# Splitting the first sums of a Strassen-Winograd token-pair product, and interleaving two accumulation chains

## The chip, the cores and the metric

The kernel runs on one core of one Trainium2 chip. The metric is the device time of one launch in microseconds (us), as the median of several runs of the same program. All traces are of single profiled executions of that program.

## The reference

Four batches, 8 heads of 40 features, 768 tokens. First an mLSTM cell over the tokens, then a block that mixes by a two-dimensional Fourier transform and ends in a small MLP. Only the MLP's second product is touched by the change:

```python
# x: (4, 768, 320), the mLSTM's output with the heads joined
X = np.fft.fft(np.fft.fft(x, axis=1), axis=2)
u = x + np.real(X)
un = (u - mean(u)) / np.sqrt(var(u) + 1e-06)          # over the 320 features
ch = np.maximum(un @ w_ch1, 0.0) @ w_ch2              # 320 -> 1280 -> 320
out = u + ch
```

## The kernel before

Everything is fp32. A token block is 128 tokens; a batch has six of them, in two groups (`gr` 0 and 1) of three. The whole program is one hand-written plan: `at(slot, phase, fn, args)` files a function under a slot and a phase, and `run()` calls them in sorted order, so the order on each engine is the order of these keys. Within a slot the phases are EVAC 0, FILL 1, MAIN 2, FILL_PE 3. The engines then run their own queues in order, and wait for each other on semaphores.

**First MLP product (the "sets").** For batches 1 to 3 `mlp_block` takes two of the ten hidden blocks of 128 features at a time, for both groups, as a 2x2 Strassen-Winograd scheme in four steps. There are five such sets, `i` = 0 to 4, so `mlp_block` fills four slots for each set and the last set ends at slot `s`. In a set TensorE fills four PSUM banks (line 897, the tails of the 320 features on line 902). ScalarE copies some of the results to the hidden tiles (lines 915, 919, 924), VectorE adds others onto them (`add`, line 906): one addition in step 1 and three at the end of step 3. The hidden tile of the fourth kind is written by ScalarE with its relu straight from PSUM (line 932). The other three kinds get their relu in place (`mlp_relu_in_place`, line 936), one after each of the next three slots, and after the last set all three in a row in slot `s`, phase EVAC.

The hidden tiles are `hid[gr, r]`, four of them, each holding five feature blocks (one for each set) by 384 tokens (three token blocks). `A11, A12, A21, A22` are the slices of `hid[1,1], hid[1,0], hid[0,1], hid[0,0]` for one pair of token blocks.

**Second MLP product (the "pairs").** `mlp_out_pair(b, n, step)` takes pair `n` of three: one token block of group 1 and one of group 0, again as a Strassen-Winograd scheme of seven products of five matmuls each (`product`, line 999, one matmul for each feature block, 128x160 out). They alternate between two PSUM banks: `x` is bank (n) % 2 and `y` is the other one. Step 0 makes two products straight from hidden tiles: A11 into `x` and A12 into `y`. Step 1 adds the product of the sum S2 onto `x`, and starts `y` anew with S1; step 2 adds S3 onto `x` and S4 onto `y`; step 3 adds A22 onto `x`. After each product VectorE takes the bank's contents onto the residual (`residual`, line 949), since every partial total is one that some output wants. So the next product on a bank waits for the residual before it, and VectorE's queue order decides when that is.

**The four sums.** `hidden_sums(n, which, f0, f1)` (line 985, VectorE) makes S1 = A21 + A22, S2 = S1 - A11, S3 = A11 - A21, S4 = A12 - S2 over the feature blocks `f0` to `f1`. For pairs 1 and 2 they are made whole (128x640), planned inside steps 2 and 3 of the pair before. For pair 0 they are made in two parts: blocks 0 to 3 (128x512) in the last set's steps, S1 and S2 ahead of the three additions of step 3 and S3 and S4 behind them; and block 4 (128x128) once the last relus are in.

Between the pairs' steps, batches 1 and 2 also run the next batch's work: Fourier products (`pz` line 686, `pu` line 729, `put` line 772) and the mLSTM (scores line 465, `mlstm_weigh` on VectorE line 471). After batch 3's sets there is nothing but pairs.

Of the kernel before, what the change touches and what calls it, by code (L numbers as in the profile page):

```python
# [26 lines left out]
NFF = DFF // L  # L27
# [23 lines left out]
def kernel(  # L51
# [33 lines left out]
    def bank(name, shape, n=None):  # L85

        return ps_m.tile(shape, FP, name=name, tag=f"pm{next(turn) if n is None else n}")
# [34 lines left out]
    def at(slot, phase, fn, *args):  # L122
        plan.setdefault((slot, phase), []).append((fn, args))
# [7 lines left out]
    EVAC, FILL, MAIN, FILL_PE = range(4)  # L131
# [813 lines left out]
    def residual(b, c, cols, po):  # L945

        k = mixes[b]
        u = k.u[:, c, cols]
        nc.vector.scalar_tensor_tensor(out=u, in0=po, scalar=k.rstd[:, c:c + 1], in1=u, op0=OP.mult, op1=OP.add)  # L949

    def store(b, c):
        nc.sync.dma_start(out=out[b, c * L:(c + 1) * L, :], in_=xs[b][:, c, 0:DM])
# [20 lines left out]
    def pair_block(n, gr, r):  # L973

        i = MLP_PAIRS[n][gr]
        return hid[gr, r].rearrange("p (f t) -> p f t", t=TG * L)[:, :, i * L:(i + 1) * L]
# [10 lines left out]
    def mlp_out_pair(b, n, step):  # L987

        k = mixes[b]
        half, first, last = NFF // 2, slice(0, HALF_D), slice(HALF_D, DM)  # L990
        c1, c2 = ORDER[TG + MLP_PAIRS[n][1]], ORDER[MLP_PAIRS[n][0]]
        if step == 0:
            k.po = [bank("po", [L, HALF_D], (n + j) % 2) for j in range(2)]
        x, y = k.po
        w = {(r, side): w2_sb[:, 1 - r:NFF:2, side * HALF_D:(side + 1) * HALF_D] for r in range(2) for side in range(2)}

        def product(po, a, w, start=False):
            for f in range(half):
                nc.tensor.matmul(po, a[:, f], w[:, f], start=start and f == 0, stop=f == half - 1, skip_group_check=True)  # L999

        def s(j):
            return hsum[f"S{j}"].rearrange("p (f t) -> p f t", t=L)

        if step == 0:
            product(x, pair_block(n, 1, 1), w[0, 0], True)
            residual(b, c1, first, x)
            product(y, pair_block(n, 1, 0), w[1, 0], True)
            residual(b, c1, first, y)
        elif step == 1:
            product(x, s(2), w2x["T2"])  # L1010
            residual(b, c1, last, x)
            product(y, s(1), w[0, 1], True)
            residual(b, c2, last, y)
        elif step == 2:
            product(x, s(3), w2x["T3"])
            residual(b, c2, last, x)
            product(y, s(4), w[1, 1])
            residual(b, c1, last, y)
            store(b, c1)
        else:  # L1020
            product(x, pair_block(n, 0, 0), w2x["T4"])
            residual(b, c2, first, x)
            store(b, c2)
# [3 lines left out]
    def plan_mlp(b, s):  # L1027
        groups = range(NT // TG)
        for i in range(NFF // 2) if b > 0 else ():
            for step in range(4):  # L1030
                at(s, MAIN, mlp_block, b, i, step)
                s += 1
            end = i == NFF // 2 - 1
            for n, (gr, f) in enumerate(((1, 2 * i + 1), (1, 2 * i), (0, 2 * i))):
                at(*((s, EVAC) if end else (s + n, MAIN + 0.5)), mlp_relu_in_place, gr, f)
        for gr in groups if b == 0 else ():
            for f in range(NFF):
                at(s, MAIN, mlp_in, b, gr, f)
                s += 1
                if f % 2:  # L1040
                    at(s, EVAC, mlp_relu, b, gr, f - 1)
                    at(s, EVAC, mlp_relu, b, gr, f)
        if b > 0:
            for j in range(1, 5):
                at(s - 1, FILL + 0.3 if j < 3 else FILL_PE + 0.3, hidden_sums, 0, (j,), 0, NFF // 2 - 1)
            at(s, EVAC, hidden_sums, 0, (1, 2, 3, 4), NFF // 2 - 1, NFF // 2)
        for n in range(TG) if b > 0 else ():
            for step in range(4):
                at(s, MAIN, mlp_out_pair, b, n, step)
                if n < TG - 1 and step > 1:  # L1050
                    for j in (2 * step - 3, 2 * step - 2):
                        at(s, MAIN + 0.6, hidden_sums, n + 1, (j,))
                s += 1
        for gr in groups if b == 0 else ():
            for i in range(TG):
                for half in range(2):
                    at(s, MAIN, mlp_out, b, gr, i, half)
                    s += 1
                at(s, EVAC, mlp_store, b, gr, i)
# [6 lines left out]
    def plan_batch(b, s_mlstm, s_mix, s_mlp):  # L1066
        plan_mlstm(b, s_mlstm)
        done = [s_mlstm + 3 * (j + NT // 2) + 7 for j in range(NT // 2)]
        assert s_mix >= done[-1] and s_mlp >= s_mix + 9
        late = [s_mlp + 2 * c for c in range(TG)]  # L1070
        if b == 0:
            feat = [s_mix + 1, s_mix + 1, s_mlp + 3]
            turn = [s_mix + 2, s_mix + 3, s_mix + 4]
            add = turn + [s_mlp, s_mlp + 4, s_mlp + 6]
            late = [s_mlp + 2, s_mlp + 5, s_mlp + 7]
        else:
            feat = [s_mix + c for c in ((3, 4, 6) if b == 1 else (3, 4, 7))]
            add = [s_mix + c for c in ((4, 4, 5, 6, 7, 7) if b == 1 else (4, 4, 5, 6, 8, 9))]
            turn = [s_mix + c for c in ((5, 6, 6) if b == 1 else (6, 7, 8))]
            late = [s_mix + c for c in ((7, 8, 8) if b == 1 else (9, 10, 10))]  # L1080
            at(s_mlp, EVAC + 0.5, mlp_sums)
        plan_mix(b, s_mix, done, feat, add, turn + late)
        at(s_mlp + NFF, FILL + 0.6, mix_rstd, b)
        plan_mlp(b, s_mlp)
# [143 lines left out]
```

## Time and profile before

| | us |
|---|---|
| median of 4 runs | 423.45 |
| lowest and highest of the runs | 422.83 and 423.79 |
| the profiled execution's own time | 423.8 |
| its span, first to last instruction | 422.1 |
| TensorE busy in the span | 409.0 |
| VectorE busy | 287.5 |
| ScalarE busy | 189.7 |
| GpSimd busy | 112.3 |
| line 999 from hidden tiles, 180 instructions (90 matmuls) in all | 26.2 |

In the profile's rows PE is TensorE's matmuls, PEld its weight loads, DVE is VectorE, ACT is ScalarE, POOL is GpSimd, SP issues DMAs. An fp32 matmul is two instructions, so ten matmuls stand as "x20". A row's duration runs to the end of the last one's drain, so back-to-back rows overlap a little: twenty instructions of line 999 follow each other in 2.72 us and last 2.98 us with the drain. The granted TensorE clock is 1.000 over the whole span. The bracket at the end of a row is the engine's idle time before it, and what ended it.

### The profile page before, as it was taken

The numbers are of one execution on the slowest core, as the hardware profiler recorded it, in microseconds if no ns is written. First come the engines' busy times: TensorE is split into PE (matmuls) and PEld (weight loads), VectorE is DVE, ScalarE is ACT, GpSimd is POOL, SyncE is SP. The second block draws the span as 40 slices with busy tenths as digits, with TensorE's granted clock in tenths as the row PEclk, the third lists the DMA queues.
The fourth block names the chain that finished last, engine by engine and source line by source line (L and its number), as shares of the span: only waits on it lengthen the run. The fifth ranks groups of instructions, "written<-read, shape, count | busy, mean of one in ns | idle before, by whom it ended". The sixth has DMA issues, their size and how long they took to land.

```text
span 422.1 us, 7995 instructions
## 1 busy us (share of the span) xinstructions
PE 409.0 (97%) x2966; PEld 302.5 (72%) x2966; DVE 287.5 (68%) x682; ACT 189.7 (45%) x493; POOL 112.3 (27%) x194
## 2 busy tenths in 40 slices
PE   8999999999999999999999999999999999999997
PEld 6877555566567778776549998976549898455996
DVE  7789894777995738778746669778654786325552
ACT  6986375686562222654455413754541123455000
POOL 5654201469331620442221530450310000020000
PEclk9999999999999999999999999999999999999999
DMA  7899298556765154276100444300000000000010
GB/s 224 284 250 316 79 267 259 177 175 206 230 185 170 63 154 135 66 209 199 46 0 2 157 156 120 114 27 1 0 2 0 33 33 32 0 2 0 16 48 31
DMA packets 20549, 47.14 MB, mean 112 GB/s; under 512 B 2784, under 2 KB 9312, under 8 KB 20384
## 3 DMA queue, kind: packets, MB, share of 16 engines
q1 hardware_dynamic: 20512, 46.65, 35.5%
q8 instruction: 23, 0.38, 0.4%
q14 instruction: 14, 0.11, 0.1%
HBM read 42.52 MB, written 4.11 MB: 110 GB/s over the span
## 4 chain that ended last, share of the span: by engine, by line
PE 78%; DVE 13%; DMA 5%; ACT 3%; issue 1%; POOL 0%; DVEq 0%; ACTq 0%; SPq 0%; POOLq 0%
PE pm L897 17%; PE po L999 16%; PE po L943 8%; PE ps L465 5%; PE pm L902 5%; PE ph L486 5%; PE ph L479 4%; DMA raw<-in_w 3%; PE pm L837 3%; PE pu L729 3%; DVE S L985 2%; PE px L535 2%; PE pz L698 2%; DMA kvt<-in_kv 1%; PE put L772 1%; DVE x L949 1%
## 5 line engine op out<-in xcount | busy, mean ns | idle before, releaser
L949 DVE SCALAR_TENSOR_TENSOR x<-po,rstd,x 128x160 f32<-128x160 f32 (+1 forms) x69 | 26.9, 394 | 41.3 <-PE po L999 35.0
L906 DVE TENSOR_TENSOR h<-h,pm 128x384 f32<-128x384 f32 x60 | 30.5, 549 | 33.1 <-ACT h L919 24.8
L421 ACT ACTIVATE W<-W,colT 128x128 f32<-128x128 f32 x144 | 45.0, 396 | 0.0
L443 POOL TENSOR_SCALAR_AFFINE_SELECT W<-W 128x1024 f32<-128x1024 f32 x18 | 21.4, 1187 | 81.1 <-ACT W L421 42.0
L943 PE MATMUL po<-w_sb,h 128*128 128x320 f32 x120 | 34.4, 435 | 0.0
L471 DVE TENSOR_TENSOR W<-ps,W 128x512 f32<-128x512 f32 x48 | 30.7, 680 | 4.8 <-POOL W L443 4.6
L897 PE MATMUL pm<-uT,w_sb 128*128 128x384 f32 x90 | 32.8, 492 | 0.2 <-DVE uT L885 0.2
L837 PE MATMUL pm<-uT,w_sb 128*128 128x384 f32 x80 | 29.9, 500 | 1.1 <-DVE x L749 0.5
L777 ACT COPY uT<-put 128x384 f32<-128x384 f32 x24 | 11.2, 478 | 40.1 <-PE put L772 40.1
L943 PEld LDWEIGHTS po<-w_sb,h 128*128 128x128 f32 x120 | 22.2, 190 | 9.5 <-issue 0.8
L999 PE MATMUL po<-T,S 128*128 128x160 f32 x180 | 27.9, 302 | 0.7 <-DVE x L949 0.6
L465 PE MATMUL ps<-qk 40*128 40x128 f32 x384 | 27.8, 284 | 0.0
L999 PE MATMUL po<-w_sb,h 128*128 128x160 f32 x180 | 26.2, 301 | 1.2 <-DVE h L906 1.2
L999 PEld LDWEIGHTS po<-T,S 128*128 128x128 f32 x180 | 25.5, 190 | 2.6 <-DVE x L949 1.7
L792 POOL TENSOR_TENSOR t<-rstd 128x6 f32<-128x6 f32 x12 | 3.2, 267 | 90.3 <-DVE v L790 89.7
L999 PEld LDWEIGHTS po<-w_sb,h 128*128 128x128 f32 x180 | 24.9, 190 | 2.8 <-DVE h L906 2.4
L465 PEld LDWEIGHTS ps<-qk 40*128 40x128 f32 x384 | 23.4, 187 | 4.2 <-issue 0.7
L486 PE MATMUL ph<-W,kvt 128*41 128x128 f32 x384 | 25.8, 277 | 0.0
L524 ACT COPY h<-ph 41x512 f32<-41x512 f32 (+1 forms) x16 | 9.3, 583 | 35.6 <-PE ph L486 35.5
L431 POOL TENSOR_TENSOR qg<-qk,Gb 128x512 f32<-128x512 f32 x18 | 25.0, 1390 | 0.1
L479 PEld LDWEIGHTS ph<-qg,C 128*128 128x128 f32 x160 | 20.0, 191 | 6.6 <-issue 2.8
L897 PEld LDWEIGHTS pm<-uT,w_sb 128*128 128x128 f32 x90 | 16.2, 190 | 10.8 <-DVE h L906 1.5
(207 smaller groups left out, 863.9 us busy)
## 6 DMA issues: line engine op xcount, KB each, us to landing
W<-M_d SPq DMA_DIRECT2D x18, 512.0 KB
kvt<-in_kv SPq DMA_DIRECT2D x24, 324.0 KB
qk<-in_qkT SPq DMA_DIRECT2D x48, 160.0 KB
raw<-in_w SPq DMA_DIRECT2D x10, 640.0 KB
Gb<-G_d SPq DMA_DIRECT2D x36, 128.0 KB
so<-in_o SPq DMA_DIRECT2D x24, 160.0 KB
out<-x SPq DMA_DIRECT2D x24, 160.0 KB
ds_sb<-in_dft_s SPq DMA_DIRECT2D x1, 1155.0 KB
```

Of the source, the lines that this page charges most:

```text
L421: nc.scalar.activation(out=k.W[:, h, :], in_=M, func=AF.Exp, scale=-1.0, bias=colT[:, c, 0, b * H + h:b * H + h + 1])
L431: nc.gpsimd.tensor_tensor(out=k.qg, in0=k.qk[:, 0], in1=k.Gb, op=OP.mult)
L465: nc.tensor.matmul(k.ps[hip][:, p, :], k.qk[r, 1, p, :], k.qk[r, 0, p, :], start=True, stop=True)
L471: nc.vector.tensor_tensor(out=Wv, in0=k.ps[hip], in1=Wv, op=OP.mult)
L479: nc.tensor.matmul(k.ph[:, p, :], k.C[:, p, :], k.qg[:, p, :], start=(p == 0), stop=False, skip_group_check=True)
L486: nc.tensor.matmul(k.ph[hip * 64:hip * 64 + D1, p, :], k.v1[:, 2 * p + hip, :], k.W[:, 2 * p + hip, :], start=(c == 0 and p == 0), stop=Tr ...
L837: nc.tensor.matmul(k.pm[i], w1_sb[:, ch, f0:f0 + L], u[2 * ch], start=(ch == 0), stop=False)
L897: nc.tensor.matmul(bank, w, u, start=start, stop=True, skip_group_check=True)
L906: nc.vector.tensor_tensor(out=h, in0=h, in1=bank, op=OP.add)
L943: nc.tensor.matmul(k.po, hidden(gr, f)[:, i * L:(i + 1) * L], w2_sb[:, f, :], start=(f == 0), stop=(f == NFF - 1))
L949: nc.vector.scalar_tensor_tensor(out=u, in0=po, scalar=k.rstd[:, c:c + 1], in1=u, op0=OP.mult, op1=OP.add)
L999: nc.tensor.matmul(po, a[:, f], w[:, f], start=start and f == 0, stop=f == half - 1, skip_group_check=True)
```

## The change

Three places. (1) For pair 0 the first part of the sums covers feature blocks 0 to 2 instead of 0 to 3. S1 is made five slots before the pairs, S2 four, S3 and S4 three slots before. (2) The second part, now blocks 3 and 4 (128x256), is split: S1 and S2 after the last relus as before, S3 and S4 inside pair 0's step 0, behind its two residuals. (3) In step 0 of every pair the two products are interleaved: four matmuls into `x`, two into `y`, the fifth into `x` (the one that needs the last set's relu), its residual, and the last three into `y`.

```diff
-        def product(po, a, w, start=False):
-            for f in range(half):
+        def product(po, a, w, start=False, f0=0, f1=half):
+            for f in range(f0, f1):
                 nc.tensor.matmul(po, a[:, f], w[:, f], start=start and f == 0, stop=f == half - 1, skip_group_check=True)
...
         if step == 0:
-            product(x, pair_block(n, 1, 1), w[0, 0], True)
+
+            product(x, pair_block(n, 1, 1), w[0, 0], True, 0, half - 1)
+            product(y, pair_block(n, 1, 0), w[1, 0], True, 0, 2)
+            product(x, pair_block(n, 1, 1), w[0, 0], False, half - 1, half)
             residual(b, c1, first, x)
-            product(y, pair_block(n, 1, 0), w[1, 0], True)
+            product(y, pair_block(n, 1, 0), w[1, 0], False, 2, half)
             residual(b, c1, first, y)
...
         if b > 0:
             for j in range(1, 5):
-                at(s - 1, FILL + 0.3 if j < 3 else FILL_PE + 0.3, hidden_sums, 0, (j,), 0, NFF // 2 - 1)
-            at(s, EVAC, hidden_sums, 0, (1, 2, 3, 4), NFF // 2 - 1, NFF // 2)
+                at(s - (5, 4, 3, 3)[j - 1], FILL_PE + 0.3, hidden_sums, 0, (j,), 0, NFF // 2 - 2)
+            at(s, EVAC, hidden_sums, 0, (1, 2), NFF // 2 - 2, NFF // 2)
+            at(s, MAIN + 0.1, hidden_sums, 0, (3, 4), NFF // 2 - 2, NFF // 2)
```

The order that comes of it on VectorE, at each of the three places where sets give way to pairs (numbers are the columns of the tiles):

```
before: add 384 (step 1) | S1 512, S2 512 | three adds 384 | S3 512, S4 512, S1 128, S2 128, S3 128, S4 128 | residual x, residual y
after:  S1 384, S2 384 | add 384 (step 1) | S3 384, S4 384 | three adds 384 | S1 256, S2 256 | residual x, residual y | S3 256, S4 256
```

In batches 1 and 2 the new S1 and S2 stand behind an addition of the Fourier fold (line 644), and the new S3 and S4 stand ahead of what followed the residuals there (line 471 in batch 1). Nothing moves on the queues of ScalarE, GpSimd and SP. TensorE has the same matmuls, reordered only within step 0 of the nine pairs.

## The prediction

> **What bounds the kernel now.** I read the page first: busy times, then the chain that ended last.
>
> ```profile
> PE 409.0 (97%) x2966; PEld 302.5 (72%) x2966; DVE 287.5 (68%) x682; ACT 189.7 (45%) x493; POOL 112.3 (27%) x194
> PE 78%; DVE 13%; DMA 5%; ACT 3%; issue 1%; POOL 0%; DVEq 0%; ACTq 0%; SPq 0%; POOLq 0%
> ```
>
> TensorE is the bound, and 13% of the chain is VectorE: places where TensorE stands still for it. No matmul is added or removed, so only such places can pay. The change touches three of them, where sets give way to pairs: at 222 us (batch 1), 315 us (batch 2), 389 us (batch 3). I read the chain in order of time around the last:
>
> ```profile
> 386.10 0.48 ACT h L924
> 386.58 0.43 ACT h L936
> 387.03 0.70 DVE S L985
> 387.76 0.69 DVE S L985
> 388.45 0.48 DVE h L906
> 388.97 2.73 PE po L999 x18
> 391.69 0.28 DVE s_last L985
> 391.97 0.31 DVE x L949
> 392.32 5.71 PE po L999 x40
> ```
>
> Read it as two stops. The 512-column sums S1 and S2 wait for the relu of set 3's last hidden tile (ends 387.00), and the three additions stand behind them in VectorE's queue. The first of these empties the PSUM bank that the pair's `x` needs, so the first matmul of the pair waits for it. Then six more sums stand ahead of the residual that the S2 product waits for. The timeline gives what each could have done:
>
> ```profile
> 385.13 0.55 DVE L906 TENSOR_TENSOR h<-h,pm 128x384 f32<-128x384 f32 x1 [3.10 <-ACT h L919]
> 385.99 1.56 PE L902 MATMUL pm<-uT,w1t_sb 64*128 64x384 f32 x8
> 387.48 0.91 PE L897 MATMUL pm<-m,w_sb 128*128 128x384 f32 x2
> 388.43 0.49 ACT L932 ACTIVATE h<-pm 128x384 f32<-128x384 f32 x1 [1.43 <-PE pm L897]
> 388.97 0.40 PE L999 MATMUL po<-w_sb,h 128*128 128x160 f32 x1 [0.57 <-DVE h L906]
> ...
> 389.41 1.35 ACT L936 ACTIVATE h<-h 128x384 f32<-128x384 f32 x3 [0.49 <-DVE h L906]
> 391.89 0.86 DVE L949 SCALAR_TENSOR_TENSOR x<-po,rstd,x 128x160 f32<-128x160 f32 x2
> 392.32 1.62 PE L999 MATMUL po<-T,S 128*128 128x160 f32 x10 [0.37 <-DVE x L949]
> ```
>
> Batch 2, in the same chain, has the first stop, but not the second, since 1.37 us of Fourier products lie ahead of the S2 product:
>
> ```profile
> 314.56 0.69 DVE S L985
> 315.26 0.48 DVE h L906
> 315.78 2.98 PE po L999 x20
> 318.76 1.37 PE pz L686 x8
> ```
>
> In batch 1 mLSTM scores lie between, and the timeline shows no idle bracket on any of its rows:
>
> ```profile
> 221.50 1.16 PE L465 MATMUL ps<-qk 40*128 40x128 f32 x16
> 222.59 2.98 PE L999 MATMUL po<-w_sb,h 128*128 128x160 f32 x20
> ```
>
> **The change part by part.** Times are those of the profiled execution (423.8 us of its own, span 422.1); the median of the runs, 423.45, lies 0.35 lower, and I subtract from the median.
>
> *Earlier sums, batch 3.* S1 and S2 over 384 columns go behind set 3's additions (end about 382.0), S3 and S4 behind set 4's first addition (385.13 to 385.68). Additions of 384 columns take 0.55, the 512-column sums 0.69, the 128-column ones 0.28. So S1 and S2 end by about 383.1, in what was 3.10 us of idle time. S3 and S4: 385.68 + 2 x 0.55 = 386.78, or about 386.63 at the starts that independent sums show in this trace (each 0.08 before its predecessor's end). When can the three additions start? In set 3 they started at 380.54 for tails that began at 379.60: 0.94 after. Set 4's tails begin at 385.99, so 386.93; VectorE is then free, with 0.15 to 0.3 to spare. That is 1.44 earlier than 388.37, and they are done by 388.41.
>
> Then TensorE need not stop. The last set product starts at 387.48; elsewhere in the sets such a pair of instructions is followed 0.75 later (381.09 to 381.84), and by another form (the scores, 220.65 to 221.50) 0.85 later. I take 0.85: the pair starts at 388.33 instead of 388.97. Gain 0.64 (0.74 at the other end).
>
> *The second stop, batch 3.* The relus now wait for no addition; they stand behind line 932, which still starts at 388.43. ScalarE starts such instructions about 0.37 after a PSUM read and 0.41 after a relu: relus from 388.80, 389.21 and 389.62, the last ending at 390.15. The 256-column S1 needs it (A22). Its length, between 0.28 and 0.69, is 0.42: S1 390.18 to 390.60, S2 390.64 to 391.06, `x`'s residual from 390.98 (0.08 overlap, as before). From residual to matmul took 391.89 to 392.32, 0.43: so the S2 product starts at 391.41 instead of 392.32. Gain 0.91, the first stop's 0.64 included: TensorE is through with step 0 at 388.33 + 2.72 = 391.05, so a stop of 0.36 stays, now behind the last relu and two sums. S3 and S4 over 256 columns (0.84) follow the residuals and are done by about 392.7; their products start after 394.1.
>
> *Interleaving.* Matmuls come 0.272 apart. The fifth `x` matmul is the seventh issued: its hidden tile is due at 388.33 + 6 x 0.272 = 389.96, and its relu ends at 389.33. The last `y` matmul is issued at 390.78, its relu ends at 389.74. `x`'s result is there about 0.30 after issue (so `y`'s residual ran in batch 1: issue over at 225.31, residual at 225.61), that is at 390.53, ahead of VectorE's 390.98. So the interleaving costs nothing here. It gives little either, since the relus come earlier anyway; as a guard against late relus it has 0.54 more room.
>
> *Batch 2.* The same first stop: 315.78 becomes 315.14, gain 0.64. S2 ends near 317.9 and the residual by 318.2, while the Fourier products keep TensorE until 319.33. From there to the end the chain runs through matmuls, residuals and the next batch's mixing, each fed by this stream (none of it starts from a DMA), so I carry the 0.64 to the end.
>
> *Batch 1.* No stop, no gain. Line 471, two instructions, stands behind S3 and S4 and would start at 226.62 instead of 226.31. Behind it on VectorE is a residual at 228.34, with 0.4 to spare, and its reader on TensorE, line 486, runs at 234.74. Cost nothing; 0.3 if that cover were gone.
>
> *Pairs 1 and 2.* `y` now starts after four `x` matmuls instead of five, and needs the bank of the pair before. In batch 3 pair 1: 399.22 + 1.09 = 400.31, where that bank's residual ends at 400.33: a wait of under 0.1. Behind it step 0 would end at 402.0, and VectorE lets the next product go only at 402.15 anyway. Hidden; pair 2 has the same numbers (a stop of 0.2 covers it). In batch 1 pair 2: 258.13 against 258.01, no wait. `x`'s residual comes 0.54 later in each: in batch 2 pair 2 it would run from 346.67 to 347.05, for a product at 347.62. Hidden. Bounds for all nine pairs: a gain of nothing, a loss of 0.1 each where no cover is, of which I book zero.
>
> *Same work.* Eight sums before and after, 0.97 us for each split one before (0.69 + 0.28) and 0.97 after (0.55 + 0.42).
>
> *A rule against the trace.* On this trace the third sum of the second stage starts 0.60 after the second, which lasts 0.68. The Trainium skill ("VectorE: DVE Perf Modes", The DRAIN you can't avoid) says that the next instruction starts only once the pipe is empty. By it S3 and S4 end at 386.78, still ahead of the additions, and the residual starts at 391.06: a gain of 0.83 instead of 0.91. I take the trace; the rule makes the sum 1.47.
>
> Sum: 0.64 + 0.91 = 1.55, so 423.45 - 1.55 = 421.9 us, 0.37% faster. About 0.2%, 0.85 us, is what a measurement of this kernel can tell from no change.
>
> **The rivals.**
>
> *Only batch 3 pays* (0.12). Batch 2's 0.64 is swallowed between 316 and 357 us, where VectorE's mixing is the chain for some stretches (333.8 to 337.8, 350.5 to 353.2). For it: 13% of the chain. Against: each stretch starts from a matmul's end. 422.5.
>
> *The wait only changes place* (0.10). VectorE reaches the additions no sooner, because the sums put ahead of them run late, or S1's wait for the last relu grows: the first stop goes, the second takes it up, and batch 3 gives 0.2 or less. With batch 2's 0.64: 422.7.
>
> *Switching banks costs TensorE time* (0.08, the slower end). Each pair's step 0 changes accumulators three times instead of once: 18 more changes. Where the form of matmul changes, rows show 0.10 (225.31 to 225.41); a stream that restarts shows 0.26 of fill (2.98 for 2.72). It decides from 0.09 a change, where 18 x 0.09 eats the 1.55. At 0.26, less the 0.4 that two stops hide: 4.3 - 1.55 = +2.7, 426.2. Against: twenty instructions with a change in the middle follow in 2.72, exactly twice the 1.36 of ten without. So a change shows nothing today.
>
> *The change does not do what it says*: excluded by the instruction order, which shows the moves.
>
> **How the numbers follow.** The forecast has 0.70, and its own range is 421.3 to 422.4: the starts by 0.1 each way, the rule's 0.08, and 0.3 for the medians. To the other cases the range reaches up to 423.0; below, to 421.1, for the 0.74 at both stops and batch 1's earlier relus. Faster by over 0.2% (under 422.6): nearly all of the forecast, half of the first rival and some of the second, 0.78. Within it 0.13. Slower 0.09.
>
> **What would show it.** Right: no bracket ahead of the first line 999 row after the sets in batches 2 and 3, the three additions 0.94 after the tails' first row, line 936's three relus right behind line 932, a remaining bracket near 0.36 ahead of the S2 product in batch 3, and 0.6 and 0.9 us less between fixed points. Wrong: the bracket ahead of the pair stays or moves whole to the S2 product; step 0's twenty instructions take over 2.8 us from start to start; or batch 2's shift is gone by 357 us.

## The result, and the profile after

The changed kernel takes 421.65 us (median of 33 runs, 420.16 to 422.98), the kernel before 423.3 us (median of 52). The ratio is 0.9958, with a 95% interval of 0.9949 to 0.9967: 0.42% faster, or 1.8 us, with 1.4 to 2.2 in the interval (the two medians lie 1.65 apart). The forecast was 421.9.

The page of the changed kernel, the two rows that answer to those of before:

```profile
PE 407.5 (97%) x2966; PEld 301.8 (72%) x2966; DVE 289.0 (69%) x682; ACT 189.3 (45%) x493; POOL 112.9 (27%) x194
...
PE 84%; DVE 10%; ACT 3%; DMA 1%; issue 1%; POOL 0%; ACTq 0%; DVEq 0%; POOLq 0%
```

VectorE's busy time is no shorter, but its share of the chain is down from 13% to 10%. The stops removed are under 2 us, half a per cent of the span, so most of that shift comes from elsewhere, and no run here shows from where. The same goes for the span. It is 418.8 us, 3.3 less than before, and 1.57 of it lies ahead of batch 1's first pair (start 221.02 instead of 222.59). That is no work of the change: the same 1.57 stands already in the sets (line 902 at 204.59 instead of 206.16), ahead of the first sum that was moved (214.02). In the ten profiles of this case the pair's start lies anywhere from 221.0 to 223.5. So kernels are compared here from that start to the last S2 product of the run (batch 3, pair 2): 189.38 us before, 187.68 after, 1.70 less.

The chain in order of time around batch 3's switch from sets to pairs, changed kernel:

```profile
385.18 0.86 PE pm L897 x2
...
386.06 0.49 ACT h L932
...
386.96 0.83 ACT h L936 x2
...
387.82 0.43 DVE S L985
...
388.62 0.39 DVE x L949
...
389.05 9.96 PE po L999 x70
```

No addition (line 906) is on it here any more. What holds the S2 product is relus, S1, S2, residual, in that order. The timeline of the same place shows both stops:

```profile
382.76 0.55 DVE L906 TENSOR_TENSOR h<-h,pm 128x384 f32<-128x384 f32 x1 [2.04 <-ACT h L919]
...
383.23 0.55 DVE L985 TENSOR_TENSOR S<-h,h 128x384 f32<-128x384 f32 x1
...
383.70 0.55 DVE L985 TENSOR_TENSOR s_last<-h,S 128x384 f32<-128x384 f32 x1
...
384.57 1.48 DVE L906 TENSOR_TENSOR h<-h,pm 128x384 f32<-128x384 f32 x3 [0.32 <-PE pm L902]
...
385.11 0.91 PE L897 MATMUL pm<-m,w_sb 128*128 128x384 f32 x2
...
385.86 2.88 PE L999 MATMUL po<-w_sb,h 128*128 128x160 f32 x20
...
386.45 1.34 ACT L936 ACTIVATE h<-h 128x384 f32<-128x384 f32 x3
387.82 0.42 DVE L985 TENSOR_TENSOR S<-h,h 128x256 f32<-128x256 f32 x1 [1.77 <-ACT h L936]
...
389.05 1.63 PE L999 MATMUL po<-T,S 128*128 128x160 f32 x10 [0.31 <-DVE x L949]
```

The three additions find VectorE idle (0.32 us) and wait for TensorE, no longer the reverse. The pair's first matmul has no bracket; it follows the last set product by 0.75 instead of 1.49. The bracket of the second stop is 0.31 instead of 0.37, and VectorE idles 1.77 us for the last relu ahead of the S1 that this stop waits for.

Batch 2, timeline of the kernel before:

```profile
314.29 0.91 PE L897 MATMUL pm<-m,w_sb 128*128 128x384 f32 x2
...
315.78 2.98 PE L999 MATMUL po<-w_sb,h 128*128 128x160 f32 x20 [0.58 <-DVE h L906]
...
318.60 0.51 PE L686 MATMUL pz<-ds_sb,fe 128*128 128x193 f32 x2
...
319.97 1.52 PE L999 MATMUL po<-T,S 128*128 128x160 f32 x10
```

And of the changed kernel:

```profile
312.77 0.91 PE L897 MATMUL pm<-m,w_sb 128*128 128x384 f32 x2
...
313.52 2.88 PE L999 MATMUL po<-w_sb,h 128*128 128x160 f32 x20
...
316.24 0.51 PE L686 MATMUL pz<-ds_sb,fe 128*128 128x193 f32 x2
316.28 0.88 DVE L949 SCALAR_TENSOR_TENSOR x<-po,rstd,x 128x160 f32<-128x160 f32 x2
...
317.61 1.52 PE L999 MATMUL po<-T,S 128*128 128x160 f32 x10
```

No idle bracket on TensorE, and the residuals lie beside the Fourier products. From the last set product to the S2 product it takes 4.84 us (312.77 to 317.61), instead of 5.68 (314.29 to 319.97).

Where the 1.70 came from, in each kernel's own times:

| stretch | before | after | difference |
|---|---|---|---|
| batch 1, pair 0: first matmul to S2 product | 4.19 | 4.19 | 0 |
| batch 1, pair 2: first matmul to S2 product | 6.49 | 6.54 | +0.05 |
| batch 2: last set product to S2 product of pair 0 | 5.68 | 4.84 | -0.84 |
| batch 2's S2 product to batch 3's last set product | 67.51 | 67.50 | -0.01 |
| batch 3: last set product to S2 product of pair 0 | 4.84 | 3.94 | -0.90 |
| batch 3, pairs 1 and 2: first matmul to S2 product, each | 2.93 | 2.93 | 0 |

Batch 2's gain is carried through the 67.5 us of mixing and sets that follow. That stretch takes 67.50 to 67.53 in all ten profiles, so single profiles of such a stretch agree to a few hundredths.

### The profile page after: what moved, and what is told of

It is laid out like the page before. It is cut to its first block, busy times and chain, and to the rows that moved or that the text cites. A ratio compares the mean times of both kernels' runs of the same rounds, so it can differ in the third digit from the quotient of the medians.

```text
span 418.8 us, 8001 instructions
## 1 busy us (share of the span) xinstructions
PE 407.5 (97%) x2966; PEld 301.8 (72%) x2966; DVE 289.0 (69%) x682; ACT 189.3 (45%) x493; POOL 112.9 (27%) x194
## 4 chain that ended last, share of the span: by engine, by line
PE 84%; DVE 10%; ACT 3%; DMA 1%; issue 1%; POOL 0%; ACTq 0%; DVEq 0%; POOLq 0%
PE pm L897 17%; PE po L999 17%; PE po L943 8%; PE pm L902 5%; PE ps L465 5%; PE ph L486 5%; PE pm L837 5%; PE ph L479 4%; PE pu L729 3%; PE px L535 2%; PE pz L698 2%; PE put L772 2%; PE pm L841 1%; DMA raw<-in_w 1%; PE pz L686 1%; PE pc L496 1%
```

## The experiments

Theory: the gain is VectorE's queue, cleared ahead of the additions (batches 2 and 3) and shortened ahead of a residual (batch 3). Rivals: the interleaving carries it; or it is the early making of the sums as such that pays, in both places. "From start to end" below means from batch 1's first pair to the last S2 product in the profile, as above.

| run | time, us | ratio to before, 95% interval | from start to end | against before |
|---|---|---|---|---|
| before | 423.3 | | 189.38 | |
| the change | 421.65 | 0.9958 (0.9949 to 0.9967) | 187.68 | -1.70 |
| e1 sums only | 422.25 | 0.9961 (0.9948 to 0.9975) | 187.80 | -1.58 |
| e2 interleaving only | 423.63 | 1.0001 (0.9988 to 1.0015) | 189.43 | +0.05 |
| e3 S3, S4 ahead | 422.44 | 0.9970 (0.9956 to 0.9983) | 188.36 | -1.02 |
| e4 whole sums, late | 423.33 | 0.9988 (0.9975 to 1.0002) | 188.48 | -0.90 |
| e5 relu order | 420.91 | 0.9939 (0.9922 to 0.9956) | 187.32 | -2.06 |
| e6 block 3 early | 421.18 | 0.9949 (0.9931 to 0.9967) | 187.45 | -1.93 |
| e7 relu order, pair 0 | 421.14 | 0.9944 (0.9929 to 0.9959) | 187.23 | -2.15 |
| e8 all | 420.42 | 0.9940 (0.9919 to 0.9961) | 186.71 | -2.67 |

The ratios of e1 to e4 (22 runs each) are to a kernel before of 423.6, those of e5 to e8 (6 runs each) to one of 423.47. The intervals are 0.6 to 0.9 us each way, so differences of tenths are read from the traces.

**e1: the sums alone.**

```diff
# against the changed kernel
-            product(x, pair_block(n, 1, 1), w[0, 0], True, 0, half - 1)
-            product(y, pair_block(n, 1, 0), w[1, 0], True, 0, 2)
-            product(x, pair_block(n, 1, 1), w[0, 0], False, half - 1, half)
+            product(x, pair_block(n, 1, 1), w[0, 0], True)
             residual(b, c1, first, x)
-            product(y, pair_block(n, 1, 0), w[1, 0], False, 2, half)
+            product(y, pair_block(n, 1, 0), w[1, 0], True)
```

> The sums moved as in the change, step 0 left as five x and then five y matmuls. Theory (the gain comes from clearing VectorE's queue ahead of the three additions and ahead of the residual): the fifth x matmul is due 1.09 us after the pair's start and its relu ends 1.12 after it, so batch 2 loses 0.1 to 0.2 of its 0.84, batch 3 loses nothing because a stop of 0.31 lies behind it, and the 0.05 that the interleaving costs in batch 1 comes back: 1.5 to 1.7 us under the kernel before, some 421.7. Rival (taking the relus' block last is what pays): the wait for the relu replaces the first stop in batches 2 and 3, over 0.5 us each: 0.7 us under the kernel before or less, 422.6.

1.58 us less from start to end. Batch 2's step 0, timeline of e1:

```profile
315.02 3.05 PE L999 MATMUL po<-w_sb,h 128*128 128x160 f32 x20
315.22 0.49 ACT L932 ACTIVATE h<-pm 128x384 f32<-128x384 f32 x1 [1.43 <-PE pm L897]
315.61 1.34 ACT L936 ACTIVATE h<-h 128x384 f32<-128x384 f32 x3
```

Twenty instructions last 3.05 instead of 2.88: the fifth `x` matmul is due at 315.02 + 1.09 = 316.11 and its relu ends 0.53 after 315.61, at 316.14. The wait is longer than these 0.03, since it holds the weight load in front of the matmul, which starts at 316.17 and was due some 0.13 ahead of the matmul. So the interleaving is worth 0.17 in batch 2. It costs 0.05 in batch 1, which e1 gets back (6.49), and makes no difference in batch 3, where e1 has the same 3.19 from the pair's start to the S2 product as the change. The rival, that taking the relus' block last is what pays, falls.

**e2: the interleaving alone.** The sums' lines are those of the kernel before:

```diff
# against the changed kernel
-                at(s - (5, 4, 3, 3)[j - 1], FILL_PE + 0.3, hidden_sums, 0, (j,), 0, NFF // 2 - 2)
-            at(s, EVAC, hidden_sums, 0, (1, 2), NFF // 2 - 2, NFF // 2)
-            at(s, MAIN + 0.1, hidden_sums, 0, (3, 4), NFF // 2 - 2, NFF // 2)
+                at(s - 1, FILL + 0.3 if j < 3 else FILL_PE + 0.3, hidden_sums, 0, (j,), 0, NFF // 2 - 1)
+            at(s, EVAC, hidden_sums, 0, (1, 2, 3, 4), NFF // 2 - 1, NFF // 2)
```

> The interleaving alone, with the sums as before. Theory: the first stop stays (additions behind the sums, 0.6 to 0.7 ahead of the pair in batches 2 and 3), so does the second (0.37): no gain, a loss of 0.05 in batch 1; 423.3 to 423.4, inside 0.2% of the kernel before. Rival (the interleaving carries part of the gain by itself): 0.4 us or more faster.

No change (1.0001), and +0.05 from start to end. Both stops stand, to the hundredth, in its timeline of batch 3:

```profile
388.29 2.98 PE L999 MATMUL po<-w_sb,h 128*128 128x160 f32 x20 [0.57 <-DVE h L906]
...
391.65 0.54 PE L999 MATMUL po<-T,S 128*128 128x160 f32 x2 [0.37 <-DVE x L949]
```

**e3: S3 and S4 ahead of the residuals.**

```diff
# against the changed kernel
-            at(s, MAIN + 0.1, hidden_sums, 0, (3, 4), NFF // 2 - 2, NFF // 2)
+            at(s, EVAC, hidden_sums, 0, (3, 4), NFF // 2 - 2, NFF // 2)
```

> The change, but S3 and S4 over the last two blocks ahead of pair 0's two residuals instead of behind them. Theory (in batch 3 the residual behind the sums sets when the S2 product starts): two more sums, 0.42 + 0.34 = 0.76, delay it: the stop ahead of the S2 product in batch 3 grows from 0.31 to about 1.07; in batch 2 the residual would end at about the time that TensorE gets there, no loss; 0.75 us slower than the changed kernel, 0.9 to 1.0 under the kernel before. Rival (the last relu, not VectorE's queue, sets that start): under 0.2 slower than the changed kernel.

The timeline of e3 in batch 3:

```profile
391.11 0.42 DVE L985 TENSOR_TENSOR S<-h,h 128x256 f32<-128x256 f32 x1
391.45 0.42 DVE L985 TENSOR_TENSOR s_last<-h,S 128x256 f32<-128x256 f32 x1
391.78 0.86 DVE L949 SCALAR_TENSOR_TENSOR x<-po,rstd,x 128x160 f32<-128x160 f32 x2
...
392.21 1.08 PE L999 MATMUL po<-T,S 128*128 128x160 f32 x6 [0.98 <-DVE x L949]
```

The stop grows from 0.31 to 0.98, and the stretch from start to end by 0.68 against the change. Batch 2 does not notice (4.08 from the pair's start to the S2 product, 4.09 in the changed kernel). With the first stop gone, but S3 and S4 of the last two blocks ahead of the residual, all that is left of batch 3's 0.90 is 0.23 (387.60 to 392.21, 4.61 instead of 4.84). So putting S3 and S4 behind the residuals is worth 0.67 of it. The rival, that the last relu and not VectorE's queue sets the start, falls.

**e4: nothing made in the sets.**

```diff
# against the changed kernel
-            for j in range(1, 5):
-                at(s - (5, 4, 3, 3)[j - 1], FILL_PE + 0.3, hidden_sums, 0, (j,), 0, NFF // 2 - 2)
-            at(s, EVAC, hidden_sums, 0, (1, 2), NFF // 2 - 2, NFF // 2)
-            at(s, MAIN + 0.1, hidden_sums, 0, (3, 4), NFF // 2 - 2, NFF // 2)
+            at(s, EVAC, hidden_sums, 0, (1, 2))
+            at(s, MAIN + 0.1, hidden_sums, 0, (3, 4))
```

> Nothing of pair 0's sums made in the sets: S1 and S2 whole (128x640) behind the additions and the last relus, S3 and S4 whole behind the residuals; the interleaving as in the change. Theory: the first stop is gone all the same, since no sum stands ahead of the additions, so batch 2 keeps its 0.84 (its residual ends 0.1 to 0.2 before TensorE needs it); batch 3 pays 0.82 + 0.83 instead of 0.42 + 0.42 behind the last relu: 0.8 slower than the changed kernel, 0.9 under the kernel before. Rival (making parts early is what pays in both places): no gain is left, 423.2.

In the trace it is as the theory has it: 0.90 under the kernel before and 0.80 over the change. Batch 2 keeps its whole gain (4.08 from the pair's start to the S2 product), with no sum made early at all. Batch 3 pays for the whole sums behind the last relu. Batch 2 (the first two lines) and batch 3 in e4's timeline:

```profile
314.61 2.88 PE L999 MATMUL po<-w_sb,h 128*128 128x160 f32 x20
...
318.69 1.54 PE L999 MATMUL po<-T,S 128*128 128x160 f32 x10
...
388.91 0.82 DVE L985 TENSOR_TENSOR S<-h,h 128x640 f32<-128x640 f32 x1 [1.77 <-ACT h L936]
389.77 0.82 DVE L985 TENSOR_TENSOR S<-S,h 128x640 f32<-128x640 f32 x1
...
390.95 1.62 PE L999 MATMUL po<-T,S 128*128 128x160 f32 x10 [1.11 <-DVE x L949]
```

From the last set product (386.21) to the S2 product batch 3 takes 4.74, so 0.10 of its 0.90 is left. The rival falls in batch 2 and stands in batch 3: there the parts made early are worth 0.80, by what they take from behind the last relu. The timed ratio, 0.9988, is weaker evidence: its interval, +0.1 to -1.1 us, holds both the 0.90 and the rival's nothing. The traces tell them apart, the times alone do not.

**e5: the relus' order.** What is the stop made of that the change leaves? Only the last set's relus change order:

```diff
# against the changed kernel
-            for n, (gr, f) in enumerate(((1, 2 * i + 1), (1, 2 * i), (0, 2 * i))):
+            last = ((1, 2 * i), (0, 2 * i)) if not end else ((0, 2 * i), (1, 2 * i))
+            for n, (gr, f) in enumerate(((1, 2 * i + 1), *last)):
```

> The changed kernel, with the last set's relus in place in another order: the hidden tile that S1 needs (A22's) second, the one that the last y matmul needs third. Theory (the stop that the change leaves in batch 3 is the chain last relu, S1, S2, residual, S2 product): S1 starts 0.41 earlier, the residual 0.41 earlier and 0.1 after x's result; the S2 product starts at about the time that TensorE is through with step 0: stop gone, 0.4 to 0.47 faster than the changed kernel by the trace from batch 1's pairs to the end, 2.1 to 2.2 under the kernel before. Nothing changes in batch 2, which has no stop. Rival (the stop is VectorE's queue alone): no change against the changed kernel.

The timeline of e5 in batch 3:

```profile
388.35 1.34 ACT L936 ACTIVATE h<-h 128x384 f32<-128x384 f32 x3
389.31 0.43 DVE L985 TENSOR_TENSOR S<-h,h 128x256 f32<-128x256 f32 x1 [1.36 <-ACT h L936]
...
390.12 0.38 DVE L949 SCALAR_TENSOR_TENSOR x<-po,rstd,x 128x160 f32<-128x160 f32 x1
...
390.55 1.63 PE L999 MATMUL po<-T,S 128*128 128x160 f32 x10
```

VectorE's wait for the relu is 0.41 shorter, and TensorE has no bracket left: 2.78 from the pair's start (387.77) to the S2 product, against 3.19 and the 2.72 of no stop at all. From start to end it is 0.36 less than the change. So the stop stood on the relu that S1 needs, and VectorE's queue alone, the rival, falls.

**e6: block 3 in the idle time.**

```diff
# against the changed kernel
-            at(s, EVAC, hidden_sums, 0, (1, 2), NFF // 2 - 2, NFF // 2)
-            at(s, MAIN + 0.1, hidden_sums, 0, (3, 4), NFF // 2 - 2, NFF // 2)
+            at(s - 1, FILL_PE + 0.3, hidden_sums, 0, (1, 2, 3, 4), NFF // 2 - 2, NFF // 2 - 1)
+            at(s, EVAC, hidden_sums, 0, (1, 2), NFF // 2 - 1, NFF // 2)
+            at(s, MAIN + 0.1, hidden_sums, 0, (3, 4), NFF // 2 - 1, NFF // 2)
```

> The changed kernel, with the sums of feature block 3 (128x128 each) in the 1.77 us in which VectorE idles for the last relus, so that only block 4 (128x128) is left behind them. Theory: S1 and S2 behind the last relu take 0.28 each instead of 0.42; the residual starts 0.27 earlier and the stop in batch 3 shrinks from 0.31 to 0.04: 0.3 faster than the changed kernel by the trace, 2.0 under the kernel before. Rival (with a floor other than these sums, such as x's result at 0.3 after its issue): under 0.1.

The timeline of e6 in batch 3:

```profile
385.99 2.88 PE L999 MATMUL po<-w_sb,h 128*128 128x160 f32 x20
...
388.92 1.62 PE L999 MATMUL po<-T,S 128*128 128x160 f32 x10
```

From the pair's start to the S2 product it takes 2.93 instead of 3.19, and 0.23 less from start to end: the sums behind the last relu count as well, by their length. It is a second way to most of the same 0.4.

**e7: interleaving for pair 0 only, on top of e5.**

```diff
# against e5
+            cut = (half - 1, 2) if n == 0 else (half, 0)
-            product(x, pair_block(n, 1, 1), w[0, 0], True, 0, half - 1)
-            product(y, pair_block(n, 1, 0), w[1, 0], True, 0, 2)
-            product(x, pair_block(n, 1, 1), w[0, 0], False, half - 1, half)
+            product(x, pair_block(n, 1, 1), w[0, 0], True, 0, cut[0])
+            product(y, pair_block(n, 1, 0), w[1, 0], True, 0, cut[1])
+            product(x, pair_block(n, 1, 1), w[0, 0], False, cut[0], half)
             residual(b, c1, first, x)
-            product(y, pair_block(n, 1, 0), w[1, 0], False, 2, half)
+            product(y, pair_block(n, 1, 0), w[1, 0], cut[1] == 0, cut[1], half)
```

> As the kernel with the other relu order, and the interleaving kept for pair 0 only, since pairs 1 and 2 have no relu to wait for. Theory: batch 1's pair 2 no longer waits 0.05 for the bank of y; in batch 3 the waits of 0.18 for that bank in pairs 1 and 2 go too, but lie beside VectorE's residual, so nothing more: 0.05 faster than that kernel. Rival (the waits in batch 3 count): 0.4 faster than that kernel.

Batch 1's pair 2 is back at 6.49. In batch 3 the stretch of pairs 1 and 2 is 2.93, as with the interleaving: the waits for the bank of `y` were hidden there. From start to end it is 0.09 less than e5, for 0.05 expected.

**e8: S3 and S4 of batch 3's pairs 1 and 2 behind the residuals, on top of e7.**

```diff
# against e7
-                        at(s, MAIN + 0.6, hidden_sums, n + 1, (j,))
+                        at(s if j < 3 or b < 3 else s + 1, MAIN + (0.6 if j < 3 or b < 3 else 0.1), hidden_sums, n + 1, (j,))
```

> As the last, and in batch 3 S3 and S4 for pairs 1 and 2 behind the two residuals of those pairs' step 0 instead of ahead of them. Theory (the S2 products of pairs 1 and 2 wait for a residual behind two sums of 0.73 each; from the pair's start to the S2 product 2.93 instead of 2.72): both stops of 0.21 go, 0.42 faster than the last kernel, 2.6 us under the kernel before, some 420.7. Rival (the 0.21 is fill of the stream, not a wait): no change against the last.

Pair 1 of batch 3 in the timeline of e7, then in that of e8:

```profile
396.31 2.88 PE L999 MATMUL po<-w_sb,h 128*128 128x160 f32 x20
...
399.24 1.38 PEld L999 LDWEIGHTS po<-T,S 128*128 128x128 f32 x10 [0.29 <-DVE x L949]
399.24 1.63 PE L999 MATMUL po<-T,S 128*128 128x160 f32 x10
...
400.71 1.52 PE L999 MATMUL po<-w_sb,S 128*128 128x160 f32 x10
```

```profile
396.41 2.88 PE L999 MATMUL po<-w_sb,h 128*128 128x160 f32 x20
...
398.99 1.41 PEld L999 LDWEIGHTS po<-T,S 128*128 128x128 f32 x10
399.12 1.52 PE L999 MATMUL po<-T,S 128*128 128x160 f32 x10
...
400.48 1.52 PE L999 MATMUL po<-w_sb,S 128*128 128x160 f32 x10
```

Both stretches go from 2.93 to 2.71, and 0.52 goes from start to end. With a median of 420.42 it is the fastest kernel of the case, 0.60% under the kernel before (interval 0.39% to 0.81%). By the times alone it is not told apart from e5; by the traces it is 0.61 ahead of it.

## Why the prediction was right, point by point

*The first stop.* The additions came 0.95 after the first tail (0.94 forecast), with 0.32 to spare (0.15 to 0.3). The pair's start moved by 0.74, not 0.64. Of the two precedents for what follows a set product, 0.75 and 0.85, the nearer one was 0.75 (312.77 to 313.52); the 0.85 belongs to the scores. Further, the working counted the start alone, but step 0 itself got shorter: in batch 2 it took 2.82 from its first matmul to the Fourier products, and takes 2.72 now. So batch 2 gave 0.84, and was under-sized by 0.20.

*The second stop.* Forecast 0.91 for batch 3 in all, measured 0.90. The relus and sums set the S2 product's start, as the working had it, so the earlier start of the pair changed nothing there. That the bracket left, 0.31, is near the forecast 0.36 is luck: the 0.36 was counted from the end of step 0's issue, and counted so the stop measured 0.47 (385.86 + 2.72 = 388.58, to 389.05), longer by the 0.10 that the pair started earlier. The bracket counts from the end of the row, 0.16 later. S1 waited for the last relu as forecast, and e3, e5 and e6 show every link of that chain: the queue, the relu and the sums' length.

*The interleaving.* It was forecast to cost nothing and to give little. It gives 0.17 in batch 2 (e1) and costs 0.05 in batch 1. The wait for `y`'s bank in batch 3 was forecast under 0.1 and is 0.18. The working compared the matmul's time with the residual's end, but the wait sits on the weight load, which comes earlier. From the changed kernel's timeline, pair 1 of batch 3:

```profile
395.95 3.06 PE L999 MATMUL po<-w_sb,h 128*128 128x160 f32 x20
396.68 0.38 DVE L949 SCALAR_TENSOR_TENSOR x<-po,rstd,x 128x160 f32<-128x160 f32 x1
...
397.11 1.66 PEld L999 LDWEIGHTS po<-w_sb,h 128*128 128x128 f32 x12 [0.16 <-DVE x L949]
```

The residual ends at 397.06, the weight load starts 0.05 later, and its matmul, due at 397.04, comes 0.18 late. Batch 1 shows the same: by the forecast the matmul had 0.1 to spare, but its weight load stands at 256.50 instead of 256.43, 0.05 behind the end of the residual. In batch 3 the wait was hidden, as forecast, by VectorE's queue (e7), but with 0.03 to spare (395.95 + 2.72 + 0.18 = 398.85, for 398.88) instead of 0.15.

*Batch 1*: no gain, as forecast, and line 471 found its cover, but not by the sum in the working. S3 took 0.73 there instead of 0.42 (224.35), beside a GpSimd instruction (line 437, 224.06 to 224.80); that this is why was not tried. So line 471 started 0.60 later against the pair's start, not 0.31, and 0.16 of VectorE's 0.75 us of idle time behind it is left. The reserve covered a delay of twice the forecast size; that it was large enough was luck.

*The sum*: 0.84 + 0.90 - 0.05 = 1.69, for 1.55 forecast and 1.70 in the trace. The mechanism was right in both places; the term that was too small is batch 2's.

*The rule weighed.* S4 started 0.08 before S3's end (383.70, S3 until 383.78), as in the trace before. The additions had room by either reading. The residual started at 388.62, 0.08 before the end of S2 (388.70), so batch 3 came to the trace's 0.91 rather than the rule's 0.83. The working quoted only half of the rule. The same section of the Trainium skill ("VectorE: DVE Perf Modes", The DRAIN you can't avoid) adds that an instruction that is not held starts earlier, so the page, read whole, need not stand against these rows.

*The rivals.* Only batch 3 pays: no, batch 2's shift stands 67 us on. The wait changes place: it did not; batch 3 gave 0.90, where this rival had 0.2 or less. Switching banks costs time: step 0 of batch 2's pair 1 takes 2.71 from its first matmul to the next product with one change (330.90 to 333.61), and 2.71 with three (328.54 to 331.25).

## What to carry to other kernels

Where an engine's queue mixes work that somebody waits for with work that nobody needs yet, ask of each stop which instruction releases it, and what stands ahead of that one in its queue. Where the queue alone held TensorE up, order alone was enough: e4 moved no sum earlier and kept all of batch 2's gain. Where the chain behind the last input set the time, as in batch 3, its length counted too: without the early parts only 0.10 of the 0.90 was left. And swapping two relus took 0.41 us off the wait that remained. Where a stage has other matmuls to run meanwhile, as batch 1 has, the same queue costs nothing, so look for the stage that has none.

## What the runs showed of the hardware

A stop on TensorE cost 0.26 us more than its idle bracket, in two places. In batch 2 a stop with a bracket of 0.58 was worth 0.84. In batch 3 of the changed kernel the stop with a bracket of 0.31 stretches step 0 and the S2 product behind it to 4.65 (385.86 to 390.51), instead of 2.72 + 1.36 = 4.08: 0.57. The stops that e8 takes away from e7 had no bracket on the matmul's row at all, and each was worth 0.22 in its stretch and 0.11 in the S2 product behind it.

Of the 0.26, 0.16 is a matter of counting: the bracket begins where the row before it ends, and a row of twenty instructions lasts 2.88 where the next could follow after 2.72. The other 0.10 is lost in the first product behind the stop: 2.82 instead of 2.72 for step 0 of batch 2, 1.47 (399.24 to 400.71) instead of 1.36 (399.12 to 400.48) for the S2 product of e7 and e8. The row of 2.98, described ahead of the prediction as 2.72 with the drain, has both parts in it. In the lines of e7 and e8 the weight load starts together with its matmul behind the stop, and 0.13 ahead of it in the stream that runs on; that the tenth is spent there was not tried. It is not bound to a stop either: in batch 1, behind the scores and without a bracket, step 0 takes 2.82 in both kernels.
